# Expert 5's rows fetched from its own fill, the rows of experts 5 and 6 turned by VectorE and ScalarE, expert 5's first layer by seven products, and the last short list made one expert earlier

## The chip, the cores and the metric

The kernel runs on one core of a Trainium2 chip, as one program. The metric is the device time of one execution in microseconds, the median of several. The core has five engines with queues of their own: TensorE (PE in the profile, its weight loads PEld), VectorE (DVE), ScalarE (ACT), GpSimd (POOL) and SyncE (SP). Each works through its own instructions in the order in which they stand, and waits on semaphores for the others.

## What is computed

A linear attention block over 4 batches, 8 heads, 768 steps and a head size of 48, and behind it a layer of 8 experts over the 3072 resulting rows of 384 numbers:

```python
for t in range(S):                                   # attention: y is x after a reshape to (3072, 384)
    cur = np.einsum('bhd,bhe->bhde', u[None] * kt, vt)
    y[:, :, t] = np.einsum('bhd,bhde->bhe', rt, state + cur)
    state = w[None, :, :, None] * state + np.einsum('bhd,bhe->bhde', kt, vt)
...
logits = x @ w_gate
order = np.argsort(-logits.flatten())
for idx in order:                                    # greedy, 384 rows for each expert
    tok, e = (int(idx) // E, int(idx) % E)
    if assigned[tok] >= 0 or counts[e] >= cap:
        continue
    assigned[tok] = e
    counts[e] += 1
...
for e in range(E):
    h = np.maximum(x[mask] @ w1[e], 0.0)             # mask = assigned == e; w1[e] is 384 x 1024
    out[mask] = h @ w2[e]                            # w2[e] is 1024 x 384
```

Everything is float32.

## The kernel before

The attention part fills the first part of the span. It writes the rows to memory and the gate's scores to LG, and one "early" expert is picked while it still runs: 256 of that expert's 384 rows are worked through at once, and its last 128 rows come at the very end. The experts between are worked through one at a time. I call the work on the n-th of them pass n, with n from 1 to 7, and pass 8 is the early expert's short rest.

**Finding lists.** The greedy rule is replaced by one search per expert: among the rows that are left, the search finds which expert fills up first, at which score, and which rows it gets. `likely_steps` (L1079) is one search. It has three rounds, each of a comparison on VectorE, three small matmuls (`counts`, L980), sums on VectorE, one more small matmul (L991) and again sums on VectorE, and ends with two small matmuls into `st_ps` (L1136, L1137). It is a generator with seven yields. `leave` (L1062) takes the found rows and the expert out of the scores, and only then can the next search start. `tokens` (L1445) makes a list of row numbers out of the result (VectorE, the matmuls `some_ps` at L1441 and `list_ps` at L1466). The last list of the seven is what remains (`remainder`, L1375), without a search.

**Fetching.** `fetch` (L1562) gathers the expert's rows into `xg` (three indirect DMAs on POOL, L1557) and loads its two weight matrices of 1.5 MB each (SP, L1550). It needs the list and the expert's number. If the early expert itself fills up among the lists, it has to be passed over: `choose` (L1168) then puts the following list in the place of the one found. So a fetch with `choose` waits for the following search, too. Lists taken without `choose` are marked `first=True` in `book` (L1146), and the check `found` (L1009) makes the program run its second arm (everything once more by a general way) if the early expert was among them.

**One pass.** The rows are turned (`xT`), go through the first layer (`hidden`, L1672, 24 matmuls of 384 columns; or `hidden_by_seven`, L1624, which builds the layer from seven products of half blocks, 44 matmuls of 192 columns, with sums of blocks of `w1` and `xT` made on VectorE at L1603 and L1614, products kept by ScalarE at L1640 and additions on VectorE at L1648), and through the second layer: `seven` (L1735, seven products for the first 256 rows, then `result` at L1808 for the last 128) or, in passes 6 and 7, `fifteen` (fifteen products). There are two sets of buffers (`turns`, one for even and one for odd n), so the next expert's rows and weights come while this one is worked on.

**Turning the next rows.** Near the end of pass n the rows of expert n + 1 are turned. `turned` (L1566) does it with nine transposes on TensorE (L1572) and three copies on ScalarE (L1573). `turned_by_quarters` (L1580) does it with three transposes of 32 x 32 blocks on VectorE (L1586) and sixteen copies on ScalarE (L1593), each of which moves blocks of all three gathered chunks to one quarter of the partitions. Which way is taken stands in `BY_QUARTERS` (L1526), by the number of the expert whose rows are turned, with the products of the pass after which so many steps of it are issued. Which experts' first layer goes by seven products stands in `FIRST_BY_SEVEN` (L1820); for these the first weight matrix is loaded first.

**Order.** The program text is written as one sequence, and a planner that is part of the language orders each engine's queue from it by its own costs: what stands earlier in the text comes first where it is ready, and an engine with nothing ready takes later work. Within `run` (L1822) the generator `later` (L2009) is pulled: at the start of pass n it is pulled until it gives the next fetch, so all that stands before that fetch has precedence over pass n's own work; then, as the pass proceeds, it is pulled as many times as the last argument of `x.run` says (2 where nothing is said), spread between three quarters of the first layer and the end of the second.

In the kernel before, `later` goes like this. The fetches of experts 2, 3 and 4 follow right behind the search that gives their list. For experts 5, 6 and 7 the following search (for 7: none is needed, the remainder is) comes before the fetch. Passes 1, 2 and 3 have 5, 7 and 9 pulls, in which the following search is done in pieces. After the last fetch but one, `found` and the short list of the early expert's rest stand at the start of pass 7.

Of the kernel before, what the change touches and what calls it, by code (L numbers as in the profile page):

```python
# [1488 lines left out]
def rwkv5_eagle_then_base_layer_balanced(  # L1489
# [14 lines left out]
    E, _, F = moe_w1.shape  # L1504
# [12 lines left out]
    walk = Assignment(ctx, tc, LG, CAP, C)  # L1517
# [5 lines left out]

    class Experts:

        BY_QUARTERS = {2: {3: 3, 4: 5, 6: 5}, 3: {2: 1, 3: 2, 4: 5, 6: 5}, 4: {2: 1, 3: 2, 4: 5, 6: 5}, 7: {5: 5, 9: 11}, 8: {5: 6, 9: 10}}  # L1526

        def __init__(self):
            self.turns, self.copied, self.added = [], None, None
# [10 lines left out]
        def load_weights(self, n, fmax):  # L1540
# [7 lines left out]
            both = (w2, moe_w2), (w1, moe_w1)  # L1548
            for t, src in both[::-1] if n in self.FIRST_BY_SEVEN else both:
                nc.sync.dma_start(t, src[ds(E - e, 1)].rearrange("o (c p) f -> p (o c) f", p=128))  # L1550
# [266 lines left out]
            nc.scalar.copy(o_sb, o_ps)  # L1817
            self.scatter(o_sb, tok[:, c:c + 1], to)

        FIRST_BY_SEVEN = 3, 6, 7  # L1820

        def run(self, ahead, later, rows, pulls={}, xT=None):  # L1822
            xT, lead = xT or self.turn(ahead), True
            row_sums = weight_sums = None
            while ahead:
# [6 lines left out]
                ahead = next((a for a in later if a), None)  # L1832
                after = ahead and ahead[0] in self.FIRST_BY_SEVEN and ahead[2].shape[1] == NC
                late, lead = lead and not many, False
# [15 lines left out]

                by_quarters = ahead and ahead[0] in self.BY_QUARTERS and whole
                turning = by_quarters and self.turned_by_quarters(ahead[0], ahead[1], ahead[2].shape[1])

                def turn_some(step):
                    nonlocal xT
                    for _ in range(self.BY_QUARTERS[ahead[0]].get(step, 0)):
                        xT = next(turning, xT)
# [12 lines left out]
                def progress(t):  # L1870
                    nonlocal weight_sums
                    if after and t > 1.1 and not weight_sums:
                        weight_sums = self.weight_sums(ahead[3])
                    while due and t > due[0]:
                        due.pop(0)
                        next(later, None)
                        if many and not due and not turning:
                            turn()
# [61 lines left out]
    with ExitStack() as whole:  # L1940
        x = Experts()
        for i in range(2):
            x.open(whole, i)
        rows = iter(out_rows)
        have = {}
        first = walk.new_outs()
        with ExitStack() as part:
            mild = Mild(tc, r, k, v, w, u, moe_w_gate, x_dram, LG, ident, walk)
            mild.open(part)
            epool = part.enter_context(tc.tile_pool(name="f_early", bufs=1))  # L1950

            def on_star(star):
                have["w"] = x.load_weights(0, star)

            def on_tokens(tok):
                have["x"] = x.gather(0, tok, N - N // C), tok

            early = walk.early(on_star, on_tokens)
            U = mild.N
            steps = [(U - 7, "first"), (U - 7, "paired"), (U - 6, "paired"), (U - 5, "products"), (U - 5, "paired"),  # L1960
                     (U - 3, "turning"), (U - 3, "turning"), (U - 3, "states"), (U - 2, "states"),
                     (U - 1, "rows"), (U - 1, "last")]

            def step(n, at):
                for _ in range(steps.count((n, at))):
                    next(early)

            with tc.manual_schedule():
                one, last = mild.run(step)
                NE = walk.EARLY // 128  # L1970
                pieces = x.early(mild.ps, epool, *have["w"], *have["x"], rows, have)

                def go(m):
                    for _ in range(m):
                        next(pieces, None)

                go(NE)
                mild.rows_out((U - 2,), one)
                mild.rows_out((U - 1,), last)
                go(2)  # L1980
                search = walk.likely_steps(**first, on_fmax=lambda fmax: have.update(v=x.load_weights(1, fmax)))
                for m in (1, 5, 2, 5, 2, 6, 5):
                    next(search)
                    go(m)
                next(search, None)
                walk.between = lambda: go(1)
                tok = walk.tokens(first["place"])
                walk.between = lambda: None
                xg = x.gather(1, tok)
                to = walk.in_order(tok)  # L1990
                walk.leave(first)
                next(early)
                have["to"] = walk.in_order(have["x"][1])
                second = walk.new_outs()
                search = walk.likely_steps(**second)
                ahead = 1, xg, to, *have["v"]
                turned = x.turned(ahead, lambda c: mild.ps.tile([128, KD, 128], F32, name="xT_ps",
                                                                tag=("kT_ps", "rT_ps")[c % 2]))
                go(7)
                next(search)  # L2000
                go(2)
                next(search)
                for m in (0, 1, 99):
                    go(m)
                    xT = next(turned)
                walk.book(first, first=True)
        x.open_rest(whole, reuse_waits="tile")

        def later():  # L2009
            yield from search  # L2010
            walk.bound(ident)
            now = second
            for n in range(2, 5):
                walk.book(now, first=True)
                yield x.fetch(n, now["fmax"], walk.tokens(now["place"]))
                walk.leave(now)
                yield
                now = walk.new_outs()
                yield from walk.likely_steps(**now)
            was = now  # L2020
            walk.book(was)
            walk.leave(was)
            for n in range(5, E):
                rest = n == E - 1
                yield
                if rest:
                    yield
                    now = walk.remainder()
                else:
                    now = walk.new_outs()  # L2030
                    yield from walk.likely_steps(**now)
                walk.book(now, surely=rest)
                walk.choose(was, now)
                yield x.fetch(n, was["fmax"], walk.tokens(was["place"]))
                if not rest:
                    walk.leave(now)
                was = now
            yield
            yield
            tc.mark_branch_hint_location("whole")  # L2040
            have["ok"] = walk.found()
            yield x.fetch(E, walk.star, walk.tokens(walk.star_place, 1))

        x.run(ahead, later(), (a for a in [*out_rows[2:NT - 1], None]),
              {1: 5, 2: 7, 3: 9}, xT)

    with tc.If(have["ok"] < 1, label="whole", preferred_fallthrough_block=False):
        with ExitStack() as arm:
# [2 lines left out]
        with ExitStack() as arm:  # L2051
            x = Experts()
# [40 lines left out]
```

## Time and profile before

| | |
|---|---|
| time, median of three | 391.88 us (391.51 to 393.09) |
| the profiled execution | 393.56 us, its span 391.8 us |
| granted TensorE clock, mean | 0.994 |
| first matmul of passes 2, 3, 4, 5, 6 | 185.00, 217.18, 248.90, 283.37, 315.57 us |
| first matmuls of passes 7 and 8 | 343.93 and 373.86 us |
| last matmul ends | 385.0 us |

The profile's times count from the start of the span. A row of the order of time has the start, the length, the engine, the line, the operation, what is written from what is read (with sizes) and how many instructions were merged in the row; in brackets at the end stands how long the engine was idle before it, and what it waited for. Matmuls overlap, so a row's length is a little more than the distance to the next. A float32 matmul is two instructions. A row of the table of groups has count, busy time and mean nanoseconds after the bar. A row of the table of windows has the stretch, its length, the busy time and number of instructions of PE, PEld, DVE, ACT and POOL, then the granted TensorE clock, the share of the DMA engines and the GB/s that they moved.

### The profile page before, as it was taken

To read this page: it belongs to the slowest core of one execution; us is meant where nothing else is said; L and a number is where in the kernel's file an instruction comes from. 1 tells how busy PE (TensorE), PEld (TensorE's weight loads), DVE (VectorE), ACT (ScalarE), POOL (GpSimd) and SP (SyncE) were. 2 spreads that over 40 slices of the span, in tenths; PEclk is the share of its full clock that TensorE was granted. 3 is DMA by queue.
4 is the path that set the end of the run, shared out by engine and by line. 5 is a ranking of instruction groups with operands and counts; after the bars stand their busy time and mean duration, and the time that the engine had idled before them with its cause. 6 is when DMAs were issued, how large, how long until landed. Compare 5 with 4: busy or idle time off the path is not lost.

```text
span 391.8 us, 9825 instructions
## 1 busy us (share of the span) xinstructions
PE 371.6 (95%) x3738; PEld 300.9 (77%) x3738; DVE 276.9 (71%) x911; ACT 195.0 (50%) x519; POOL 145.0 (37%) x195
## 2 busy tenths in 40 slices
PE   7799999999989999999999999999899999989993
PEld 6677888888877866687577898558557889979981
DVE  6755768586884767977868949887378866995630
ACT  4997989888872311237228346321222234744620
POOL 7887978777732022022222211203113221061020
PEclk9999999999999999999999999999999999999997
DMA  7988977787582174641651550109109652281010
GB/s 144 187 178 175 223 165 174 170 178 160 135 315 82 43 248 174 224 161 43 217 184 42 172 230 23 40 4 364 56 22 326 258 181 60 56 310 42 2 63 26
DMA packets 95336, 57.36 MB, mean 146 GB/s; under 512 B 77232, under 2 KB 89520, under 8 KB 95280
## 3 DMA queue, kind: packets, MB, share of 16 engines
q1 hardware_dynamic: 91936, 47.21, 42.6%
q0 software_dynamic: 3104, 9.44, 6.9%
q8 instruction: 31, 0.51, 0.5%
q14 instruction: 25, 0.20, 0.2%
q10 hardware_dynamic: 240, 0.00, 0.0%
HBM read 47.20 MB, written 9.44 MB: 145 GB/s over the span
## 4 chain that ended last, share of the span: by engine, by line
PE 69%; issue 9%; POOL 8%; DVE 7%; ACT 3%; DMA 2%; POOLq 1%; another core or an unknown queue 0%; ACTq 0%; DVEq 0%
PE h_ps L1679 15%; PE y_ps L546 6%; PE pa_ps L1753 6%; PE o_ps L1811 5%; PE g_ps L506 5%; PE h_ps L1656 4%; PE pb_ps L1753 3%; ACT xT L1593 3%; PE e_h_ps L1923 3%; PE hb_ps L1656 3%; PE kv_ps L525 2%; PE kT_ps L459 2%; PE x_ps L597 2%; PE lg_ps L577 2%; PE p_ps L1784 2%
## 5 line engine op out<-in xcount | busy, mean ns | idle before, releaser
L1679 PE MATMUL h_ps<-xT,w 128*128 128x384 f32 (+1 forms) x264 | 73.2, 427 | 0.2 <-ACT hid L1682 0.2
L496 ACT ACTIVATE AT<-ident,dd 128x128 f32<-128x128 f32 x192 | 59.7, 393 | 2.1 <-DVE dd L449 2.1
L1679 PEld LDWEIGHTS h_ps<-xT,w 128*128 128x128 f32 x264 | 42.0, 191 | 19.9 <-issue 2.3
L1805 POOL DMA_INDIRECT out_dram<-o_all,to x16 | 20.7, 1291 | 92.1 <-DVE o_all L1793 41.3
L1682 ACT ACTIVATE hid<-h_ps 128x384 f32<-128x384 f32 (+1 forms) x40 | 17.8, 448 | 55.7 <-PE h_ps L1679 52.2
L1557 POOL DMA_INDIRECT xg<-x_rows,tok x22 | 22.5, 1023 | 61.7 <-DVE parts L968 26.3
L513 DVE COPY_PREDICATED AT<-mask,g_ps 64x512 f32<-64x512 uint8 (+1 forms) x48 | 32.4, 724 | 16.1 <-PE g_ps L506 14.4
L1811 PE MATMUL o_ps<-w,hid 128*128 128x384 f32 x96 | 33.3, 490 | 0.0
L1593 ACT COPY xT<-xq 32x288 f32<-32x288 f32 (+1 forms) x80 | 31.7, 397 | 1.7 <-DVE xq L1586 0.4
L506 PE MATMUL g_ps<-rT,kT 48*64 48x128 f32 (+1 forms) x768 | 26.3, 255 | 1.4 <-DVE AT L513 1.0
L437 POOL TENSOR_TENSOR kss<-krs,wk 128x384 f32<-128x384 f32 x24 | 24.3, 1018 | 7.5 <-DVE krs L341 4.6
L546 PE MATMUL y_ps<-AT,vts 128*64 128x128 f32 x384 | 25.7, 276 | 0.0
L1811 PEld LDWEIGHTS o_ps<-w,hid 128*128 128x128 f32 x96 | 17.5, 190 | 10.3 <-issue 1.0
L444 POOL TENSOR_TENSOR rk<-rk,u_bc 128x384 f32<-128x384 f32 x24 | 24.1, 1004 | 1.9
L443 POOL TENSOR_TENSOR rk<-krs 128x384 f32<-128x384 f32 x24 | 24.6, 1023 | 0.0
L506 PEld LDWEIGHTS g_ps<-rT,kT 48*64 48x64 f32 x768 | 20.6, 132 | 5.0 <-issue 1.0
L546 PEld LDWEIGHTS y_ps<-AT,vts 128*64 128x64 f32 x384 | 20.6, 137 | 1.0 <-issue 0.7
L478 DVE TENSOR_TENSOR rT<-rT_ps,WR 112x512 f32<-112x512 f32 x23 | 15.7, 681 | 2.8 <-PE rT_ps L459 2.7
L565 ACT COPY x<-y_ps 128x512 f32<-128x512 f32 x24 | 14.1, 586 | 7.0 <-PE y_ps L546 3.5
L449 DVE TENSOR_REDUCE dd<-rk 128x8 f32<-128x384 f32 x24 | 13.0, 543 | 6.1 <-POOL rk L444 6.0
L1644 ACT ACTIVATE hid<-kept_P 128x384 f32<-128x384 f32 x18 | 9.4, 523 | 13.5 <-DVE kept_P L1648 11.9
L546 PE MATMUL y_ps<-rT,states 48*64 48x128 f32 x320 | 16.0, 276 | 0.0
(351 smaller groups left out, 831.9 us busy)
## 6 DMA issues: line engine op xcount, KB each, us to landing
w<-in_moe_w_dram SPq DMA_DIRECT2D x18, 1536.0 KB, 11.0
krs<-in_k_dram SPq DMA_DIRECT2D x24, 192.0 KB, 3.6
krs<-in_r_dram SPq DMA_DIRECT2D x24, 192.0 KB, 4.6
vts<-in_v_dram SPq DMA_DIRECT2D x24, 192.0 KB, 3.5
x_rows<-xr SPq DMA_DIRECT2D x24, 192.0 KB, 3.7
xg<-x_rows,tok POOLq DMA_INDIRECT x22
out_dram<-o_all,to POOLq DMA_INDIRECT x16
out_dram<-o_sb,to POOLq DMA_INDIRECT x5
```

The lines of the kernel that those rows point to most:

```text
L437: self.nc.gpsimd.tensor_mul(self.kss[:, n % self.NS].rearrange("p (g h) d -> p g h d", g=2)[:, :, :, 0:D], src, self.wk.rearrange("p (g h) ...
L443: nc.gpsimd.tensor_mul(rk, self.krs[:, n % self.NK, 1, 0:H, 0:D], self.krs[:, n % self.NK, 0, 0:H, 0:D])
L444: nc.gpsimd.tensor_mul(rk, rk, self.u_bc)
L496: nc.scalar.mul(AT[:, z, a, :], self.ident, dd[:, h:h + 1])
L506: nc.tensor.matmul(g_ps[ts(i, PD), z, a, i * PD:], kT[rows, a, ts(i, PD)], rT[rows, a, i * PD:], start=True, stop=True)
L513: nc.vector.copy_predicated(out=AT[keys, :, :, steps], mask=mask, data=g_ps[keys, :, :, steps])
L546: nc.tensor.matmul(yv[q * PD:(q + 1) * PD, o // 2, o % 2, :], lhsT, rhs, start=(o // 2, q) not in seen, stop=stop, skip_group_check=True)
L1593: nc.scalar.copy(to[ts(q, 32), 0:nb, :, g, :], xq[ts(g, 32), 0:nb, :, q, :])
L1656: nc.tensor.matmul(ps[:, q, :], w[b][:, ts(p * Q + q, 128)], x[a], start=fresh, stop=(a, b) == pairs[-1], skip_group_check=True)
L1679: nc.tensor.matmul(h_ps[j][:, at], w1[:, f, ts(j, 128)], xT[:, f, at], start=(f == 0), stop=(f == KD - 1))
L1753: nc.tensor.matmul(ps, left[a][:, j, :], right[b][:, j, :], start=(j == 0 and name in ("P1", "P2", "P5")), stop=(j == KF // 2 - 1), skip_g ...
L1811: nc.tensor.matmul(o_ps, hid[:, j, ts(c, 128)], w2[:, j, :], start=(j == 0), stop=(j == KF - 1))
```

## The change

Expert 5's fetch follows right behind the search that gives its list, without `choose` (the first loop now goes to 5, the second starts with 6). The search after that is done in pieces during pass 4, which gets nine pulls; pass 3 gets eight in place of nine. Expert 6's fetch still waits for the search after its own, and that search now stands whole at the start of pass 5. The rows of experts 5 and 6 are turned by quarters. Expert 5 joins those whose first layer goes by seven products. The short list of the early expert's rest is made at the first pull of pass 6 in place of the start of pass 7; the gather that uses it stays there.

```diff
-        BY_QUARTERS = {2: {3: 3, 4: 5, 6: 5}, 3: {2: 1, 3: 2, 4: 5, 6: 5}, 4: {2: 1, 3: 2, 4: 5, 6: 5}, 7: {5: 5, 9: 11}, 8: {5: 6, 9: 10}}
+        BY_QUARTERS = {2: {3: 3, 4: 5, 6: 5}, 3: {2: 1, 3: 2, 4: 5, 6: 5}, 4: {2: 1, 3: 2, 4: 5, 6: 5}, 5: {2: 1, 3: 2, 4: 5, 6: 5}, 6: {2: 1, 3: 2, 4: 5, 6: 5}, 7: {5: 5, 9: 11}, 8: {5: 6, 9: 10}}
...
-        FIRST_BY_SEVEN = 3, 6, 7
+        FIRST_BY_SEVEN = 3, 5, 6, 7
...
             now = second
-            for n in range(2, 5):
+            for n in range(2, 6):
                 walk.book(now, first=True)
                 yield x.fetch(n, now["fmax"], walk.tokens(now["place"]))
                 walk.leave(now)
...
             was = now
             walk.book(was)
             walk.leave(was)
-            for n in range(5, E):
+            for n in range(6, E):
                 rest = n == E - 1
                 yield
...
                 was = now
+            left_over = walk.tokens(walk.star_place, 1)
             yield
             yield
             tc.mark_branch_hint_location("whole")
             have["ok"] = walk.found()
-            yield x.fetch(E, walk.star, walk.tokens(walk.star_place, 1))
+            yield x.fetch(E, walk.star, left_over)
...
         x.run(ahead, later(), (a for a in [*out_rows[2:NT - 1], None]),
-              {1: 5, 2: 7, 3: 9}, xT)
+              {1: 5, 2: 7, 3: 8, 4: 9}, xT)
```

## The prediction

> **What bounds the kernel now.** I read the page's span, busy times and chain first, then TensorE's order of time from expert 2 on.
>
> ```profile
> span 391.8 us, 9825 instructions
> PE 371.6 (95%) x3738; PEld 300.9 (77%) x3738; DVE 276.9 (71%) x911; ACT 195.0 (50%) x519; POOL 145.0 (37%) x195
> PE 69%; issue 9%; POOL 8%; DVE 7%; ACT 3%; DMA 2%; POOLq 1%; another core or an unknown queue 0%; ACTq 0%; DVEq 0%
> ```
>
> TensorE is busy 95% of the span and carries 69% of the chain. So the change is worth what it takes out of TensorE's queue plus what it removes from that queue's idle time, less the idle time that it adds. I call the work on expert n "pass n", its first matmul on TensorE Tn, and "search n" the search that fills the n-th list; a search ends at its st_ps matmul.
>
> ```profile
> 185.00 1.54 PE L1679 MATMUL h_ps<-xT,w 128*128 128x384 f32 x4
> 217.18 0.49 PE L1656 MATMUL h_ps<-xT,w 128*128 128x192 f32 x2
> 217.97 0.17 PE L1136 MATMUL st_ps<-acc,ones 128*128 128x24 bf16 x1 [0.30 <-DVE acc L1132]
> 248.80 0.17 PE L1136 MATMUL st_ps<-acc,ones 128*128 128x24 bf16 x1
> 248.90 2.82 PE L1679 MATMUL h_ps<-xT,w 128*128 128x384 f32 x8
> 262.27 0.17 PE L1136 MATMUL st_ps<-acc,ones 128*128 128x24 bf16 x1
> 275.27 0.55 PE L1572 MATMUL xT_ps<-ident,xg 128*128 128x128 f32 x3 [0.81 <-DMA xg<-x_rows,tok]
> 276.16 0.52 PE L1572 MATMUL xT_ps<-ident,xg 128*128 128x128 f32 x3 [0.35 <-DVE cnt L988]
> 276.85 0.49 PE L1572 MATMUL xT_ps<-ident,xg 128*128 128x128 f32 x3
> 283.37 2.15 PE L1679 MATMUL h_ps<-xT,w 128*128 128x384 f32 x6
> 292.56 0.17 PE L1136 MATMUL st_ps<-acc,ones 128*128 128x24 bf16 x1
> 292.61 4.12 PE L1679 MATMUL h_ps<-xT,w 128*128 128x384 f32 x12
> 296.56 0.31 PE L1441 MATMUL some_ps<-vals,row 128*128 128x48 f16 x6
> 300.13 1.46 PE L1753 MATMUL pa_ps<-w,hid 128*128 128x192 f32 x8
> 301.43 1.46 PE L1753 MATMUL pc_ps<-w,hid 128*128 128x192 f32 x8
> 307.93 0.82 PE L1572 MATMUL xT_ps<-ident,xg 128*128 128x128 f32 x6
> 308.59 0.56 PE L1753 MATMUL pa_ps<-T,hid 128*128 128x192 f32 x2
> 309.00 0.55 PE L1572 MATMUL xT_ps<-ident,xg 128*128 128x128 f32 x3
> 309.38 1.14 PE L1753 MATMUL pa_ps<-T,hid 128*128 128x192 f32 x6
> 315.57 0.90 PE L1656 MATMUL h_ps<-xT,w 128*128 128x192 f32 x4
> ```
>
> Read the starts: T2 185.00, T3 217.18, T4 248.90, T5 283.37, T6 315.57. Pass 4 takes 34.5 us and pass 5 32.2; pass 2, which turns the next rows by VectorE and ScalarE, takes 32.2. Searches 4 to 7 end at 217.97, 248.80, 262.27 and 292.56. Search 6 runs in one piece at the start of pass 4 (13.5 us after search 5) because expert 5's fetch waits for it; then expert 5's rows land so late that TensorE waits 0.81 + 0.35 us for them.
>
> **Pass 4: -2.3 us.** Expert 5's list now comes from search 5, so its fetch (three gathers on POOL, two weight loads on SP) moves from the end of search 6 to T4, ahead of search 6 on every queue. Its rows then land some 13 us earlier and can be turned by VectorE and ScalarE. TensorE loses nine transposes (0.33 us for three: 0.66 from 307.93 to 308.59 for six) and the two waits: about 1.0 + 1.16. Search 6 goes in pieces into pass 4's nine pulls. Pass 4 then has the make-up of today's pass 2: full first layer, next rows turned in quarters, next expert by seven products, a search in pieces. So I take pass 2's length, 32.2, which contains the small waits of such a pass and the added VectorE sums: -2.3. Bounds -1.2 (waits doubled) and -3.
>
> **Pass 5, TensorE's own work: -2.5 us.** The trace has two instructions for each matmul. By seven products the first layer is 88 of them with 192 columns, eight in 1.30 us (300.13 to 301.43), so 14.3; today it is 48 with 384 columns, twelve in 3.95 (292.61 to 296.56), so 15.8: -1.5. The nine transposes go: 0.66 + 0.38 = 1.0. TensorE could leave pass 5 at T5 + 29.7.
>
> **Pass 5, when expert 6's rows are ready.** Here the wait removed from pass 4 comes back, longer. Expert 6's fetch waits for search 7 (choose needs it), search 7 needs search 6's result taken out of the scores, and search 6 now runs through pass 4. Where the searches run in pieces, they end with their pass: search 4 (seven pulls) 0.8 after T3, search 5 (nine pulls) 0.1 before T4. I put search 6's end at T5 (bounds -1.5 and +0.8). Search 7 then runs in one piece as search 6 does today.
>
> ```profile
> 263.38 1.74 SPq L1550 DMA_DIRECT2D w<-in_moe_w_dram  x2
> 269.40 0.99 POOL L1557 DMA_INDIRECT xg<-x_rows,tok  x1 [6.80 <-DVE tok L1474]
> 271.96 1.09 POOL L1557 DMA_INDIRECT xg<-x_rows,tok  x1 [0.30 <-issue]
> 273.00:274.00 1.00, 1.00 (x8) 1.00 (x7) 0.55 (x2) 0.00 (x0) 0.22 (x2) 1.00 1.07 394
> 274.00:275.00 1.00, 0.46 (x6) 0.27 (x4) 0.59 (x1) 0.32 (x1) 0.81 (x1) 1.00 0.62 224
> L1648 DVE TENSOR_TENSOR kept_P<-kept_P,hb_ps 128x384 f32<-128x384 f32 x6 | 3.3, 554 | 2.2 <-PE hb_ps L1656 1.5 <-issue 0.6
> 332.84 1.49 DVE L1586 STREAM_TRANSPOSE xq<-xg 128x384 f32<-128x384 f32 x3
> 338.33 4.83 ACT L1593 COPY xT<-xq 32x288 f32<-32x288 f32 x11
> ```
>
> Step by step from T5: search 7 13.5, and 0.6 for VectorE's six additions of the seven products (0.55 each, any of them can stand ahead of a search step): T5 + 14.1. From a search's end to the last rows' landing: 276.85 - 262.27 = 14.6 in pass 4, where TensorE waited for the rows; at most 309.00 - 292.56 = 16.4 in pass 5, where the next expert's weights load as well, as they will here. I take 15.5: T5 + 29.6. Last VectorE transpose, 0.5: T5 + 30.1. Then 16 ScalarE copies, 4.83/11 = 0.44 each, 7.0 us, of which every one must be done before pass 6's first product (each fills one quarter of the partitions): T5 + 37.1, and 0.3 to hand over: **T6 = T5 + 37.4**. Today it is 32.2: **+5.2 us**, with TensorE idle for 7.7 (37.4 - 29.7). Bounds: all early (-1.5, 0, 14.6, no hand-over) T5 + 34.1; all late (+0.8, 1.5 for the additions, 16.4, a 0.5 copy between) T5 + 40. Behind the waiting transposes stand the column sums of pass 6's second layer on VectorE, needed 15 us into pass 6, and pass 5's last output copy on ScalarE: neither sets anything.
>
> The 14.6 holds a wait of the gather for the weights: issued at 269.40, its rows were waited for until 275.27, while the DMA engines moved 394 GB/s up to 274. [...]
>
> **The clock after the idle time: +1.5 us.**
>
> ```profile
> 384.00:385.00 1.00, 0.98 (x4) 0.23 (x2) 0.00 (x0) 0.00 (x0) 0.00 (x0) 1.00 0.04 8
> 387.00:388.00 1.00, 0.00 (x0) 0.00 (x0) 0.00 (x0) 0.00 (x0) 0.00 (x0) 0.63 0.52 194
> 388.00:389.00 1.00, 0.00 (x0) 0.00 (x0) 0.00 (x0) 0.00 (x0) 0.00 (x0) 0.50 0.03 11
> 1.43 2.82 PE L419 MATMUL unread_ps<-ident 128*128 128x128 f32 x12 [1.43 <-POOL ident masks.py:199]
> 12.95 0.49 PE L419 MATMUL unread_ps<-ident 128*128 128x128 f32 x3
> ```
>
> TensorE's last matmul ends at 385.0; the granted clock (eighth column) is 0.63 in the slice from 387 and 0.50 in the next: it falls to half some 2.3 us after the last work. At the start twelve 128-column matmuls take 2.82 us, 0.235 each, against 0.11 later (six in 0.66 above): TensorE begins at half speed for at least those 2.8 us, which costs 1.4 us. With 7.7 us idle I expect that once, and take 1.5 (bounds 0, the clock holds, and 2.8, twice as long). [...]
>
> **The last short list: -1.5 us.**
>
> ```profile
> 343.77 0.30 PE L1441 MATMUL some_ps<-vals,row 128*128 128x16 f16 x6
> 348.40 0.18 PE L1466 MATMUL list_ps<-part,alike 128*128 128x12 f16 x1 [1.62 <-DVE part L1457]
> ```
>
> In pass 7 TensorE waits 1.62 us for the list's sums, which stand on VectorE behind the row and result sums. The list moves into pass 6; the gather that uses it, one on POOL, stays in pass 7. The next products have their sums before that, so 1.6 + 0.2 goes. Pass 6 gets the 0.2 back and some of the wait, for VectorE is busy there too: I take -1.5, bounds 0 and -1.8. Pass 3's one pull fewer costs nothing: what it no longer holds comes first in pass 4.
>
> **Sum.** -2.3 + 5.2 + 1.5 - 1.5 = +2.9 us. The rows are of one execution of 393.56 us (span 391.8, 1.8 around it), 1.7 above the median of 391.88; on that median 2.9 gives **394.8 us**.
>
> **The rivals.** *Rows in time (faster).* If expert 6's rows are turned by T5 + 29.7, pass 5 shrinks by 2.5: -2.3 - 2.5 - 1.5 = -6.3, 385.6 us. It decides at search 6's end: it would have to come 7.7 us before T5. For it: VectorE, 71% busy, leaves gaps, and nine pulls ask for search 6 to end with the seventh product. Against it: search 5, with nine pulls today, still ends at T4. Chance 0.14. *Rows late, but less.* Search 6 ends 1.5 early, and the last rows land with the end of the weights' traffic (the DMA share falls in the slice from 274, against 276.85 where TensorE had them: some 2 us less). T6 is then near T5 + 34, and the clock may hold: -2.3 + 1.8 - 1.5 = -2.0, or -0.5 with the clock's loss: 389.9 to 391.4, give or take one. Chance 0.28. *Not what it says.* If the fifth list were the early expert's, the check at the end would fail and the whole second arm would run, hundreds of us more; but on the reference's inputs the experts fill in the order 4, 3, 7, 5, 0, 6, 2, 1, and the early one (fewest first choices, at least 224, in the first four chunks) is expert 1 with 230: the last. Chance 0.01.
>
> **How the numbers follow.** The forecast has 0.57, between +0.5 (T6 at T5 + 35) and +6.7 (T6 at T5 + 39.9, the list's gain gone or the clock's loss doubled, not all at once). Half a per cent, 2.0 us, is about what a measurement of this kernel can tell from no change. Faster: all of the first rival and a quarter of the second, 0.21. Slower: the forecast without its lowest sixth, and the third, 0.48 + 0.01, so 0.49. Same: 0.30. The range reaches from 389.2, below the second rival, to 398.6: left out are the first rival and little above.
>
> **What would show it.** T5 - T4 near 32.2 and no TensorE transposes at L1572 in passes 4 and 5; search 6's st_ps within 1.5 us of T5 and search 7's near T5 + 14; xT copies of L1593 running past pass 5's last o_ps; TensorE idle for 4 to 10 us before pass 6's first product, released by ACT xT; a granted clock under 1 in that stretch; no wait for list_ps in pass 7. The prediction is wrong if search 6 ends well before T5, if the gather lands before the weights, or if the copies are ordered ahead of the kept products and stop TensorE inside pass 5 instead.

## The result and the profile after

| | before | after |
|---|---|---|
| median of the runs | 392.05 us | 398.34 us |
| range of the runs | 391.51 to 393.09 us | 398.15 to 398.78 us |
| profiled execution | 393.56 us, span 391.8 | 398.35 us, span 396.6 |

The ratio is 1.0159, with a 95% interval of 1.0136 to 1.0182: the change makes the kernel 6.3 us slower. The forecast was +2.9 us (394.8), with 398.6 as the top of its range.

The page of the changed kernel shows nearly the same matrix work. Its chain of waits breaks off after 2% of the span and is left out.

```profile
span 396.6 us, 9916 instructions
PE 371.7 (94%) x3760; PEld 305.3 (77%) x3760; DVE 282.9 (71%) x930; ACT 209.3 (53%) x551; POOL 146.1 (37%) x195
```

TensorE is busy for 371.7 us where it was 371.6, though it lost the transposes and an eighth of one first layer: part of what it does now takes longer. The timeline of TensorE in the changed kernel shows where:

```profile
248.38 4.11 PE L1679 MATMUL h_ps<-xT,w 128*128 128x384 f32 x12
281.14 0.17 PE L1136 MATMUL st_ps<-acc,ones 128*128 128x24 bf16 x1 [0.89 <-DVE acc L1132]
281.24 0.89 PE L1656 MATMUL h_ps<-xT,w 128*128 128x192 f32 x4
294.97 0.17 PE L1136 MATMUL st_ps<-acc,ones 128*128 128x24 bf16 x1
297.38 1.46 PE L1753 MATMUL pa_ps<-w,hid 128*128 128x192 f32 x8
306.21 1.57 PE L1753 MATMUL pa_ps<-T,hid 128*128 128x192 f32 x8 [0.41 <-ACT kept_P L1758]
313.29 8.13 PE L1811 MATMUL o_ps<-w,hid 128*128 128x384 f32 x16 [5.51 <-DVE o_all L1743]
321.25 0.81 PE L1656 MATMUL h_ps<-xT,w 128*128 128x192 f32 x4
350.00 0.82 PE L1656 MATMUL h_ps<-xT,w 128*128 128x192 f32 x4
357.77 0.92 PE L1656 MATMUL h_ps<-xT,w 128*128 128x192 f32 x4 [0.87 <-DVE kept_P L1648]
```

T4, T5, T6 and T7 are 248.38, 281.24, 321.25 and 350.00; before, they were 248.90, 283.37, 315.57 and 343.93 (the last from the same view of the kernel before). Stage by stage, between the two profiled executions:

| stage | before | after | measured | forecast |
|---|---|---|---|---|
| up to T4 | 248.90 | 248.38 | -0.5 | 0 |
| pass 4 | 34.47 | 32.86 | -1.6 | -2.3 |
| pass 5 | 32.20 | 40.01 | +7.8 | +5.2 |
| pass 6 (with the clock's loss in the forecast) | 28.36 | 28.75 | +0.4 | +1.5 |
| pass 7 | 29.93 | 29.07 | -0.9 | -1.5 |
| pass 8 to the end | 17.94 | 17.53 | -0.4 | 0 |
| span | 391.8 | 396.6 | +4.8 | +2.9 |

The other 1.5 of the 6.3 us lies between executions: the profiled one of the kernel before was 1.5 us above its median, that of the changed kernel at its median. The 0.4 us behind pass 7 are not the change's either: in four runs below (the parts alone, and both mended at once) this stretch takes 18.0 us and in the eight others 17.5 to 17.6, whatever the edit.

So pass 5 is the place. TensorE waits 5.51 us there for an addition into o_all, and then does the sixteen products of o_ps in 8.13 us. In the kernel before they took 5.32:

```profile
310.36 5.32 PE L1811 MATMUL o_ps<-w,hid 128*128 128x384 f32 x16
```

The timeline of VectorE in the changed kernel shows what stands ahead of that addition:

```profile
307.96 0.58 DVE L1586 STREAM_TRANSPOSE xq<-xg 128x384 f32<-128x384 f32 x1 [3.15 <-DMA xg<-x_rows,tok]
309.70 0.58 DVE L1586 STREAM_TRANSPOSE xq<-xg 128x384 f32<-128x384 f32 x1 [0.59 <-DMA xg<-x_rows,tok]
312.41 0.58 DVE L1586 STREAM_TRANSPOSE xq<-xg 128x384 f32<-128x384 f32 x1 [2.13 <-DMA xg<-x_rows,tok]
312.92 0.32 DVE L1743 TENSOR_TENSOR o_all<-kept_P,pb_ps 128x192 f32<-128x192 f32 x1
```

VectorE waits three times for rows of expert 6, until 312.41 (T5 + 31.2), and only then adds pb_ps to o_all, which frees the PSUM buffer that o_ps needs. Only its place in the queue holds the addition back: put first, in an experiment below, it begins at 304.69, T5 + 23.6. The granted clock (the figure behind the five engines) shows why o_ps took longer:

```profile
311.00:312.00 1.00, 0.00 (x0) 0.00 (x0) 0.00 (x0) 0.00 (x0) 0.00 (x0) 0.97 0.81 310
314.00:316.00 2.00, 2.00 (x4) 1.01 (x3) 2.00 (x7) 1.95 (x5) 0.50 (x1) 0.50 0.26 98
318.00:319.00 1.00, 1.00 (x4) 0.56 (x3) 0.79 (x2) 0.95 (x3) 0.08 (x1) 0.61 0.00 0
```

It falls to half at 311.94 (0.97 is 0.06 of that us at half) and is back at 318.78. The work in between starts at 313.29, so 5.5 us of it go at half speed: 2.75 us, nearly what o_ps has grown by (2.8).

### The profile page after: what moved, and what is told of

The parts are those of the page before. It is cut to its first block, busy times and chain, and to the rows that moved or that the text cites. A ratio compares the mean times of both kernels' runs of the same rounds, so it can differ in the third digit from the quotient of the medians.

```text
span 396.6 us, 9916 instructions
## 1 busy us (share of the span) xinstructions
PE 371.7 (94%) x3760; PEld 305.3 (77%) x3760; DVE 282.9 (71%) x930; ACT 209.3 (53%) x551; POOL 146.1 (37%) x195
## 5 line engine op out<-in xcount | busy, mean ns | idle before, releaser
L1679 PE MATMUL h_ps<-xT,w 128*128 128x384 f32 (+1 forms) x216 | 55.4, 410 | 0.0
L1805 POOL DMA_INDIRECT out_dram<-o_all,to x16 | 20.9, 1308 | 91.5 <-DVE o_all L1793 23.1
L1593 ACT COPY xT<-xq 32x288 f32<-32x288 f32 (+1 forms) x112 | 45.5, 406 | 10.0 <-DVE xq L1586 8.4
L1557 POOL DMA_INDIRECT xg<-x_rows,tok x22 | 22.2, 1008 | 75.3 <-DVE parts L968 32.4
L1679 PEld LDWEIGHTS h_ps<-xT,w 128*128 128x128 f32 x216 | 33.8, 191 | 15.1 <-issue 0.8
L513 DVE COPY_PREDICATED AT<-mask,g_ps 64x512 f32<-64x512 uint8 (+1 forms) x48 | 32.4, 725 | 16.0 <-PE g_ps L506 14.3
L1811 PE MATMUL o_ps<-w,hid 128*128 128x384 f32 x96 | 36.7, 526 | 5.5 <-DVE o_all L1743 5.5
L1682 ACT ACTIVATE hid<-h_ps 128x384 f32<-128x384 f32 (+1 forms) x32 | 14.0, 438 | 41.4 <-PE h_ps L1679 39.6
L1811 PEld LDWEIGHTS o_ps<-w,hid 128*128 128x128 f32 x96 | 18.6, 204 | 17.1 <-DVE o_all L1743 6.0
L1644 ACT ACTIVATE hid<-kept_P 128x384 f32<-128x384 f32 x24 | 12.6, 523 | 19.5 <-DVE kept_P L1648 19.0
L565 ACT COPY x<-y_ps 128x512 f32<-128x512 f32 x24 | 14.1, 587 | 5.6 <-PE y_ps L546 4.3
```

The source lines that it names most:

```text
L513: nc.vector.copy_predicated(out=AT[keys, :, :, steps], mask=mask, data=g_ps[keys, :, :, steps])
L1557: nc.gpsimd.indirect_dma_start(out=xg[:, c, :], out_offset=None, in_=x_dram[0:within, :], in_offset=bass.IndirectOffsetOnAxis(ap=tok[:, 0, ...
L1593: nc.scalar.copy(to[ts(q, 32), 0:nb, :, g, :], xq[ts(g, 32), 0:nb, :, q, :])
L1679: nc.tensor.matmul(h_ps[j][:, at], w1[:, f, ts(j, 128)], xT[:, f, at], start=(f == 0), stop=(f == KD - 1))
L1805: nc.gpsimd.indirect_dma_start(out=to, out_offset=bass.IndirectOffsetOnAxis(ap=tok, axis=0), in_=o_sb, in_offset=None)
L1811: nc.tensor.matmul(o_ps, hid[:, j, ts(c, 128)], w2[:, j, :], start=(j == 0), stop=(j == KF - 1))
```

## The experiments

Two theories at the start. H: the order of VectorE's queue is the cause, and with the addition ahead of the transposes the loss would mostly go. L: the rows are late, and whatever waits for them, pass 6 can't begin sooner. Each ratio is to the kernel before, run on the same chip at the same time (392.11 us beside the first four runs, 393.34 beside the next four, 392.17 beside the last four); it is not simply the quotient of two medians. T5-relative times are from each run's own profile.

### TensorE turns the rows of six

The entry of `BY_QUARTERS` alone is shown:

```diff
-  6: {2: 1, 3: 2, 4: 5, 6: 5},
```

> The changed kernel, but TensorE turns the rows of expert 6, as it did before the change. Rows of six are expected at the same moments as in the changed kernel (about T5 + 26.7, + 28.5 and + 31.2). Theory H (the order of VectorE's queue is what stops TensorE: the turning of the late rows stands ahead of the addition that frees the bank of the last o_ps): the addition is free again, but now TensorE's own transposes of the late rows stand ahead of the last product, so TensorE waits for the DMA itself until about T5 + 31; a shorter wait, since the copies by ScalarE come piece by piece. T6 about T5 + 38, 395.5 to 397.5. Theory L (lateness alone): T6 is set by the last rows at T5 + 31 plus turning and copying (about 8), so T5 + 39, 397 to 399.

Measured: 396.7 us, ratio 1.0125 (1.0105 to 1.0145). T6 is T5 + 37.5. TensorE now waits for the DMA itself, 2.51 and 1.30 us, and its clock is at half from 310.16 to 313.56. The turning of six by VectorE and ScalarE thus costs some 1.3 us here (1.0159 less 1.0125; the two intervals overlap), about a fifth of the loss. The time and T6 are those forecast under H, but the two branches lay close together. What counts against H as the whole cause is that most of the loss stays although the order that it blames is gone.

### The additions ahead of the transposes

```diff
-  6: {2: 1, 3: 2, 4: 5, 6: 5},
+  6: {6: 6},
```

> The changed kernel, but VectorE turns expert 6's rows behind the two additions of pass 5's second layer, not ahead of them. Theory H with the order as the whole cause: the last o_ps runs at once behind P4, T5 + 26.7 to + 32, and pass 6 begins when the rows are turned; if little of the copying is left by then, T6 is near T5 + 33 and the time near 391 (5.5 us of wait and 2.8 of clock gone). Theory L (lateness): o_ps runs early, but pass 6 can't begin before the last rows have landed (T5 + 31), been turned and copied (about 8): T6 about T5 + 39, the same wait now stands ahead of pass 6, and the clock falls there for 1.4 to 2.8 us: 397 to 398.5, no gain.

Measured: 398.39 us, 1.0175 (1.0144 to 1.0205): no gain against the changed kernel's 1.0159. TensorE and the clock in this run:

```profile
307.46 4.68 PE L1811 MATMUL o_ps<-w,hid 128*128 128x384 f32 x14
311.98 0.19 PE L1395 MATMUL st_ps<-sel,ones 128*128 128x48 bf16 x1
318.47 1.65 PE L1656 MATMUL h_ps<-xT,w 128*128 128x192 f32 x4 [6.29 <-ACT xT L1593]
```

```profile
314.00:316.00 2.00, 0.00 (x0) 0.00 (x0) 2.00 (x4) 1.94 (x6) 0.00 (x0) 0.86 0.90 295
320.00:322.00 2.00, 2.00 (x8) 2.00 (x7) 0.73 (x3) 0.48 (x1) 0.18 (x1) 0.50 0.26 98
322.00:323.00 1.00, 1.00 (x7) 1.00 (x6) 0.36 (x1) 0.00 (x0) 0.00 (x0) 0.87 0.00 0
```

o_ps runs at once and at full speed. The wait has moved to pass 6's first product, 6.29 us, released by ScalarE's xT copies; the clock's loss has moved to pass 6, which takes 30.7 us. H as the whole cause falls, L holds. The last transpose began at 310.77, T5 + 29.7, for rows issued at the same T5 + 20.9 as in the changed kernel, where it was T5 + 31.2. This is the forecast's own scene, and its T6 comes out as forecast: 318.47 - 281.10 = T5 + 37.4.

### The old fetch

```diff
-            for n in range(2, 6):
+            for n in range(2, 5):
...
-            for n in range(6, E):
+            for n in range(5, E):
...
-              {1: 5, 2: 7, 3: 8, 4: 9}, xT)
+              {1: 5, 2: 7, 3: 9}, xT)
```

> The changed kernel with the old order of fetches and the old pulls (expert 5 from the same fill as before); the turning by VectorE and ScalarE, the first layer of five by seven products and the last short list ahead stay. If the fetch is the costly part: rows of five land late in pass 4 again (near T4 + 27.6), T5 near T4 + 35, but the rows of six are in time for pass 6, pass 5 takes about 32 to 33 and there is no wait of over 1 us on TensorE before pass 6: 391 to 394. If the turning by VectorE costs as much by itself, with rows in time: above 396.

Measured: 397.88 us, 1.0150 (1.0129 to 1.0171), a miss of what I thought likelier. Without the new fetch the loss is nearly the same, but it lies in both passes:

```profile
277.14 2.85 PE L1811 MATMUL o_ps<-w,hid 128*128 128x384 f32 x8 [2.59 <-DVE o_all L1743]
311.69 2.20 PE L1811 MATMUL o_ps<-w,hid 128*128 128x384 f32 x6 [2.12 <-DVE o_all L1743]
```

o_ps waits for the addition 2.59 us in pass 4 (35.7 us long) and 2.12 in pass 5 (34.9), and the product behind it (pa_ps) another 0.36 and 1.00 for kept_P, which ScalarE keeps. So H's mechanism is real, twice: the addition stands behind transposes that wait for rows in both passes. The fetch is not the one cause.

### Expert 6's weights behind its rows

```diff
+            if n in (6,):
+                late = walk.most
+                with tc.issue_after(self.gathered.ins):
+                    nc.gpsimd.tensor_tensor(out=late, in0=fmax, in1=fmax, op=ADD)
+                    nc.gpsimd.tensor_tensor(out=late, in0=late, in1=fmax, op=SUB)
+                fmax = late
...
-                nc.gpsimd.indirect_dma_start(
+                self.gathered = nc.gpsimd.indirect_dma_start(
```

> The changed kernel, but the loads of expert 6's weights are issued only behind its three row gathers. If the gathers wait for the traffic of the weights (the rows took 5.8 to 7.7 us from issue to landing, at 390 to 410 GB/s): rows land 3 to 5 us sooner, about T5 + 26.5, T6 about T5 + 34 to 36, 392 to 395, unless the weights themselves come late to pass 6. If they wait for the issue by GpSimd and not for traffic: the rows land as in the changed kernel, 398, or later by what the weights lose.

Measured: 394.17 us, 1.0050 (1.0027 to 1.0073), as the first branch had it. The DMA view ends with the median us from issue to landing; the changed kernel first and this run second:

```profile
xg<-x_rows,tok POOLq DMA_INDIRECT x3, 6.2
```

```profile
xg<-x_rows,tok POOLq DMA_INDIRECT x3, 3.1
```

Issued at the same T5 + 20.9, the rows land in half the time when no weights load beside them. T6 falls to T5 + 34.6. Half of what a gather takes here is thus the weights' traffic. What is won is partly given back. The edit puts the weights' number behind GpSimd, and VectorE, which prepares it for the load, waits for that 2.55 us; the addition to o_all stands behind, and o_ps waits 0.96 us for it. VectorE's wait for that number and its sums of expert 6's first weight matrix, then TensorE:

```profile
306.71 0.14 DVE L1548 TENSOR_SCALAR number<-most 1x1 int32<-1x1 f32 x1 [2.55 <-POOL most L1546]
314.49 1.29 DVE L1609 TENSOR_TENSOR first_T<-w 128x512 f32<-128x512 f32 x2 [5.28 <-DMA w<-in_moe_w_dram]
```

```profile
316.39 0.92 PE L1662 MATMUL h_ps<-xT,w 128*128 128x192 f32 x4 [2.39 <-ACT xT L1599]
317.15 2.49 PE L1662 MATMUL hc_ps<-xT,w 128*128 128x192 f32 x8
```

The weights now come at 314.49, 1.9 us before T6, with 2.7 us of sums to make; and in this execution the clock fell to half at 317.4, behind 2.4 us of idle time: hc_ps takes 2.49 us for eight, 1.46 elsewhere. Pass 6 takes 31.7 us. That need not hold for the others: the six executions took 393.41 to 395.82 us, with mean granted clocks from 0.998 to 0.990, and the profiled one (395.32) is the one with 0.990. By an estimate from these numbers 3.4 us at half speed lower the mean by 0.004, so the fall is not in all of them.

### The parts alone

```diff
+            left_over = walk.tokens(walk.star_place, 1)
...
-            yield x.fetch(E, walk.star, walk.tokens(walk.star_place, 1))
+            yield x.fetch(E, walk.star, left_over)
```

> The kernel before with nothing but the last short list made two steps ahead. In the kernel before TensorE waited 1.62 us for VectorE ahead of that list; the matrix work of the list itself (0.3 + 0.2) stays. The prediction's step: -1.5 (0 to -1.8): 390.3 to 390.9. Rival, by the changed kernel's trace (a new wait of 0.87 for VectorE's kept_P in the same pass, the list's matrix work moved into pass 6): what is given back there leaves -0.5, 391.6.

Measured: 392.57 us, 0.9981 (0.9968 to 0.9995). The wait of 1.62 us is gone, a wait of 0.86 for kept_P (at 352.44) has come behind it. The gain, 0.77 us, is half of the forecast's -1.5 and nearer to the rival's -0.5.

```diff
-        FIRST_BY_SEVEN = 3, 6, 7
+        FIRST_BY_SEVEN = 3, 5, 6, 7
```

> The kernel before with nothing but expert 5's first layer by seven products. Matrix work of pass 5 is 1.5 us less. If nothing else sets the end of pass 5: 390.6. Rival: TensorE comes 1.5 us earlier to the rows of expert 6, which in the run with the old fetch landed 23.7 to 26.1 us behind T5, and waits for them: 391.5 to 392.5, with a DMA wait ahead of the transposes of xg in pass 5.

Measured: 392.99 us, 0.9995 (0.9979 to 1.0011): no difference, and no wait for rows ahead of the transposes of expert 6, so the rival falls, too. Pass 5's first layer just isn't 1.5 us shorter: 283.34 to 299.51 is 16.2, where the profile of the kernel before has 16.8. Search 7's matmuls stand between products of 0.16 us each now, and in the timeline a gap of some 0.15 to 0.2 us stands ahead of four of them (twice at L980, st_ps and some_ps), which is most of what is missing.

The third takes over the new loop bounds and pulls alone (the diff of the old fetch, turned round).

> The kernel before with nothing but the new order of fetches (expert 5 from its own fill) and its pulls; TensorE turns the rows of 5 and 6, first layer of 5 by eight products, list as before. If lateness of expert 6's rows is a price of the fetch alone: pass 4 gains 1.6 to 2, pass 5 grows by 5 to 6 (rows landed T5 + 26.7 to + 31.2, TensorE waits for the DMA itself), 395 to 397. If it needs the turning by VectorE to cost anything: 390 to 391.

Measured: 393.53 us, 1.0008 (0.9991 to 1.0024). The likelier branch missed: the fetch alone makes no row late. Search 6 ends at T5 - 2.8, search 7 at T5 + 11.1, the first gather is issued at T5 + 16.9, and TensorE finds the rows there when it comes at T5 + 24.6. Pass 4 takes 32.9 us. What pass 4 gains against the profile of the kernel before does not show in the median. A wait of 0.74 us for vals (VectorE's part of the next list) in pass 6 answers part of it; part may not have been there to gain in most executions (see pass 4 in the next section).

### Both mended at once

The entry of 6 out of BY_QUARTERS, and expert 6's weights behind its rows.

> The changed kernel with two things undone or mended: TensorE turns the rows of six, and expert 6's weights are loaded behind its gathers. If the two causes (rows kept back by the weights' traffic, and 16 copies by ScalarE behind VectorE's turning) are the whole loss: rows land near T5 + 25.3, + 26 and + 26.6, TensorE waits about 1 us, T6 near T5 + 32.5, weights of six landed near T5 + 32.7: 390.5 to 392. If the late weights now set pass 6 (VectorE's first sums of w for expert 6 wait for them): T6 as said but a wait of 1 to 3 us inside pass 6, 392 to 394.

Measured: 396.47 us, 1.0089 (1.0061 to 1.0118), a miss. T6 is T5 + 34.1, not 32.5: TensorE waits 0.57 and 0.41 us for rows, then 0.79 us for the weights themselves. Pass 6 then waits 1.5 us for vals and pass 7 1.2 for kept_P, both VectorE's; 0.87 of the latter stands in the changed kernel, too. So T6 comes early, and part of the lateness moves on behind it. Against the run in which TensorE turns the rows of six and the weights stay where they were (1.0125) this is lower, with intervals that overlap; it is not better than the weights behind the rows alone (1.0050).

### Combinations

None of the three parts that ran alone costs anything; the two turnings did not run alone. Four more runs separate the combinations. The changed kernel without the two turnings:

```diff
-  5: {2: 1, 3: 2, 4: 5, 6: 5}, 6: {2: 1, 3: 2, 4: 5, 6: 5},
```

> The changed kernel, but TensorE turns the rows of five and of six; the fetch, the seven products of five and the list ahead stay. What is open: the fetch alone cost nothing (1.0008), the seven products alone nothing (0.9995), the list ahead gains (0.9981), yet the changed kernel with only six given back to TensorE stands at 1.0125. Theory V (VectorE's load in pass 4: its turning of five's rows, and five's sums for seven products which can now begin there, push search 6 back, and search 7 with it): with the turning of five gone, search 6 ends 0.5 to 2.7 us earlier against T5, rows of six come that much earlier, 0.998 to 1.005. Rival S (the seven products ahead of time are what loads pass 4): search 6 still ends near T5, TensorE still waits for rows of six for 3 to 5 us: 1.008 to 1.013.

The changed kernel without the seven products of five:

```diff
-        FIRST_BY_SEVEN = 3, 5, 6, 7
+        FIRST_BY_SEVEN = 3, 6, 7
```

> The changed kernel, but expert 5's first layer by eight products, as before the change; both turnings, the fetch and the list ahead stay. Theory V with the turning as the load: search 6 still ends within 1 us of T5, and the 16 copies by ScalarE still stand between the rows of six and pass 6: 1.010 to 1.016. Rival S (the sums for seven are the load): search 6 ends 2 us or more ahead of T5, rows of six land before VectorE wants them, 0.998 to 1.004.

The kernel before with the diffs of the list and of the seven products:

> The kernel before with the seven products of five and the list ahead, nothing else: it is also the run with the old fetch without its two turnings. The parts alone gave 0.9995 and 0.9981; if they add: 0.9976 (0.996 to 0.999), faster than both kernels. The difference to the run with the old fetch (1.015) is then the price of the two turnings, 1.7% or some 6.8 us, with no new fetch at all. If instead the turnings cost only together with the fetch, the old-fetch run's loss must come from these two parts together: 1.010 to 1.015.

The kernel before with the diffs of the fetch and of the list:

> The kernel before with the new fetch and the list ahead; TensorE turns the rows, eight products for five. The parts alone gave 1.0008 and 0.9981: if they add, 0.999 (0.997 to 1.001). Pass 4 near 32.9, rows of six in time, no list wait in pass 7. Rival: the list ahead moves work into pass 6 where the fetch left VectorE late (a wait of 0.74 for vals there), and they don't add: 1.000 to 1.003.

They gave 395.20, 395.20, 391.58 and 391.76 us.

All twelve runs and the change, with the times of pass 5 from T5 in each profile:

| new fetch | list ahead | seven for 5 | turned by VectorE | ratio (95%) | search 7 ends | first gather | T6 |
|---|---|---|---|---|---|---|---|
| | x | | | 0.9981 (0.9968 to 0.9995) | 9.2 | 15.6 | 32.2 |
| | | x | | 0.9995 (0.9979 to 1.0011) | 9.0 | 14.8 | 31.6 |
| | x | x | | 0.9981 (0.9963 to 1.0000) | 9.0 | 14.8 | 31.6 |
| | x | x | 5, 6 | 1.0150 (1.0129 to 1.0171) | 10.6 | 16.9 | 34.9 |
| x | | | | 1.0008 (0.9991 to 1.0024) | 11.1 | 16.9 | 32.4 |
| x | x | | | 0.9993 (0.9974 to 1.0013) | 11.1 | 16.9 | 32.4 |
| x | x | | 5, 6 | 1.0059 (1.0037 to 1.0081) | 12.7 | 18.1 | 36.5 |
| x | x | x | | 1.0079 (1.0051 to 1.0107) | 11.7 | 19.3 | 36.6 |
| x | x | x | 5 | 1.0125 (1.0105 to 1.0145) | 13.7 | 20.9 | 37.5 |
| x | x | x | 5, 6 (the change) | 1.0159 (1.0136 to 1.0182) | 13.7 | 20.9 | 40.0 |
| x | x | x | 5, 6, additions first | 1.0175 (1.0144 to 1.0205) | 13.7 | 20.9 | 37.4 |
| x | x | x | 5, 6, weights behind rows | 1.0050 (1.0027 to 1.0073) | 13.7 | 20.9 | 34.6 |
| x | x | x | 5, weights behind rows | 1.0089 (1.0061 to 1.0118) | 13.7 | 20.9 | 34.1 |

The list with the seven products, and the list with the fetch, add as expected (0.9981 for 0.9976, 0.9993 for 0.999). The theories V and S are half right each. Without the turnings search 6 does end 2.7 us ahead of T5, as V had it, but TensorE still waits, as S had it (2.5 us, for a forecast of 3 to 5). Without the seven products the ratio falls between the two forecasts.

The table has the price of the two turnings three times. With the old fetch they take the ratio from 0.9981 to 1.0150, which is 1.7% without any new fetch; with the new fetch from 0.9993 to 1.0059 without the seven products, and from 1.0079 to 1.0159 with them. The stop inside pass 5 is there without the seven products as well:

```profile
310.23 2.20 PE L1811 MATMUL o_ps<-w,hid 128*128 128x384 f32 x6 [3.33 <-DVE o_all L1743]
```

The new fetch and the seven products cost nothing one by one. Together, with TensorE turning, they take the ratio from 0.9993 or 0.9981 to 1.0079. Where the turnings are there already, the new fetch adds nothing that can be measured (1.0150 to 1.0159). So the parts take from one slack, the time between the landing of the rows and the moment at which they are wanted. How the seven products take from it shows in TensorE's timeline. The new fetch with the list ahead leaves it no wait:

```profile
305.92 0.82 PE L1572 MATMUL xT_ps<-ident,xg 128*128 128x128 f32 x6
307.16 0.52 PE L1572 MATMUL xT_ps<-ident,xg 128*128 128x128 f32 x3
```

With the seven products of five added, and nothing else, it has three waits:

```profile
307.26 0.55 PE L1572 MATMUL xT_ps<-ident,xg 128*128 128x128 f32 x3 [1.30 <-DMA xg<-x_rows,tok]
308.65 0.52 PE L1572 MATMUL xT_ps<-ident,xg 128*128 128x128 f32 x3 [0.84 <-DVE W L1728]
309.87 0.86 PE L1572 MATMUL xT_ps<-ident,xg 128*128 128x128 f32 x3 [0.37 <-DMA xg<-x_rows,tok]
```

The gathers take the same 6.1 to 6.2 us in both; it is their issue that moved, and VectorE that moved it. The stretch from search 7's end to the first gather, without and with the seven products:

```profile
292.47:298.30 5.83, 5.83 (x28) 3.51 (x27) 5.08 (x39) 0.99 (x3) 0.23 (x2) 1.00 0.59 201
```

```profile
293.20:300.81 7.61, 7.61 (x53) 7.34 (x53) 7.61 (x42) 2.49 (x6) 0.23 (x1) 1.00 0.69 240
```

With eight products VectorE (the third busy time) makes the list almost undisturbed in 5.83 us. With seven it is busy for all of 7.61: its timeline has three additions of the first layer's products into kept_P, 0.55 us each, and the first of the second layer's sums, 0.68 us each, between the list's steps. Add 0.6 us from search 7 itself, and the gather is issued at T5 + 19.3 in place of 16.9. For 2.4 us of lateness the pass grows by 4.2 (36.6 - 32.4): 2.5 of waits and 1.7 of clock, which is at half from 309.9 to 313.3 in this run.

The turning of five by VectorE, added to that, makes search 6 end 2.8 us later against T4 (32.8 in place of 30.0), at T5 - 0.1. Three transposes take 1.6 us of VectorE's queue. The rest I did not separate, but the first_S sums for five start 29.8 us behind T4 in the changed kernel (278.19), behind ScalarE's copies, and 27.0 behind T4 without the turnings (275.82).

## Why the prediction was wrong

The sign was right, and so was much of the mechanism: rows of expert 6 late, TensorE idle, clock at half, and search 6's and 7's ends (T5 - 0.1 and T5 + 13.7) within half a us of the forecast's T5 and T5 + 14.1. One step of the path was wrong, and the size, by the steps behind it:

- **"neither sets anything"** is the step of the path that failed. Behind the transposes I named the next column sums and the last output copy, and missed the additions of pass 5's own second layer, of which one frees a PSUM buffer. TensorE stopped for 5.51 us inside pass 5, which grew by 7.8 us and not by 5.2. The last sentence of the prediction names a stop inside pass 5 as its failure, but by the copies on ScalarE, not by the transposes on VectorE. The run with the additions first shows that this step does not make the time: without the stop the ratio is no lower (1.0175 for 1.0159), and the wait stands ahead of pass 6. The forecast's T6 of T5 + 37.4 is met to the tenth there (two misses of 0.4 us, in search 7 and in the rows, cancel), and the median, 398.39, is still 3.6 us above the forecast. So the size has to come from the terms.
- **The clock, +1.5:** 2.75 in the changed kernel, the forecast's upper bound (it had 0 to 2.8), and 1.9 with the additions first. Half speed lasted 6.84 us (311.94 to 318.78) and 6.82 (315.44 to 322.26), and 3.4 us in three other runs (310.16 to 313.56 with TensorE turning six, 317.4 to 320.8 with the weights behind the rows, 309.9 to 313.3 without the turnings): two lengths, the longer twice the shorter. What sets them was not shown. The loss depends on how much of such a stretch meets work: 5.5 of the 6.84 us here, 3.8 of the 6.82 (from 318.47 on) with the additions first. I had taken half of the first 2.8 us of the start as its size, from matmuls that took twice as long there; the granted clock is 1.00 from 0 to 6 us in the profile of the kernel before, so that row did not show a fall of the clock.
- **Pass 4, -2.3:** -1.6 in the profile, because search 6 makes TensorE wait 0.89 us at T5. Part of that gain belongs to the one execution that I read. The kernel before had 1.16 us of waits at the transposes there; 0.75, 0.38 and 0.16 us stood at the same place in three runs with the old fetch and TensorE's turning (the list alone, the seven products alone, both), whose pass 4 took 34.1, 33.7 and 33.5 us, not 34.5. Against these 32.9 is a gain of 0.7 to 1.2.
- **The list, -1.5:** -0.77 us alone (0.9981). "The next products have their sums before that" was wrong: 0.86 us came back as a wait for kept_P.
- **"On that median 2.9 gives 394.8":** the terms were read in an execution 1.5 us above the median that the result then had, and added to the median. Some 0.4 to 0.9 us of that are pass 4, as far as the three runs named under pass 4 can stand for other executions. The rest is open.
- **TensorE's own work in pass 5, -2.5:** the first layer gave 0.6, not 1.5, in the run of that part alone; with the additions first, pass 5's work ends at T5 + 30.9, not 29.7. In the sum this was hidden behind the rows.
- **The rows:** 17.4 us from search 7 to the last rows in the changed kernel (312.41 - 294.97), with 15.5 forecast and 16.4 as the bound, but 15.9 with the additions first (310.77 - 294.83). The wait for the weights that the prediction reads in its 14.6 is in the runs a slowing by their traffic: from issue to landing a gather took 6.2 us beside weights and 3.1 without. It is no wait for their end: the first two sets of rows were there at 307.96 and 309.70 while the weights still moved (the DMA engines at 397 GB/s from 309 to 310, and busy until about 311.8). How they share their time between the two was not shown.

The prediction's late bound has a slip: its own terms make T5 + 40.2 or more, not 40.

In the sum, between the profiles: pass 4 +0.7 against the forecast, passes 5 and 6 with the rows, the stop and the clock +1.5, pass 7 with the list +0.6, behind it -0.4, up to T4 -0.5. That makes +4.8 out of +2.9. The other 1.5 us up to 6.3 come from the profiled execution of the kernel before.

The cause I had wrong in one more way: I put the lateness down to the order of fetches and counted the turnings as a gain. The fetch alone left the rows in time. The two turnings cost 0.7 to 1.7% in each of the three pairs of runs with and without them, also with the old fetch; the new order costs where the seven products of five come with it. What stays open: the two turnings alone, one of them with the old fetch, and an order in which the list's steps on VectorE stand ahead of the second layer's sums, with the fetch and the seven products kept. None of these was run. The versions that come out ahead of both kernels are the list ahead alone and the list with the seven products (0.9981 each, the second's interval reaching 1.0000).

## What to carry to other kernels

Taking work off the engine that bounds a kernel can cost more than the work itself: nine transposes took 1.0 us of TensorE, and the engines that got them had what TensorE needed next behind them. Parts of a change that cost nothing one by one can share one slack: write the timetable of the one chain they all lean on (here: search, list, gather, landing, turning) against the moment at which its result is wanted, and subtract each part's delay from the same slack. When work that waits for a DMA is moved to another engine's queue, list everything behind it there, also what frees a buffer of the current stage, not the next stage's needs alone: VectorE's addition began at T5 + 31.7 behind the transposes and at T5 + 23.6 put ahead of them. And read a wait that a change is to remove in several executions before it is priced.

## What the runs showed of the hardware

- In one execution (with the weights behind the rows) the clock fell to half behind an idle stretch of TensorE of 2.4 us, 313.98 to 316.39. The fall came at 317.4, a us after work had resumed, so that it does not show in the idle stretch itself, and lasted until 320.8.
- In another run the clock fell with no idle stretch longer than 1.3 us ahead of it: without the turnings TensorE was busy for 0.55, 0.35 and 0.63 us of the three us from 307 to 310, and the clock fell at 309.9.
- A gather of 128 rows took 3.1 us from issue to landing (median of three) with no weight load beside it and 6.2 beside loads, with the DMA engines at about 390 GB/s.
